# Plain products in the first quarter and a root on GpSimd, in a kernel of linear attention and two feed-forward layers

## The chip, the cores and the metric

The kernel runs on one core of a Trainium2 chip. The time is that of one execution on the device, in microseconds (us); of the kernel before three runs were made, and their median counts. The traces come from the hardware profiler: they record, for each engine, when every instruction began and how long it took.

## The reference

Four batches of eight heads, 576 tokens each and 64 wide, go through linear attention with a norm; the 2,304 rows of 512 numbers that come out go through two feed-forward layers, 512 to 2048 to 512 each.

```
kv  = einsum('bhsd,bhse->bhde', k, v)
out = einsum('bhsd,bhde->bhse', q, kv)
rms = sqrt(mean(out * out, axis=-1) + 1e-06)
x   = (out / rms * g_norm), rows of all heads side by side     # 2304 x 512
h   = x @ w_in;   g = max(h, 0) + log1p(exp(-|h|));  x = g @ w_out    # layer 1
h   = x @ w_in2;  g = h if h > 0 else exp(h) - 1;    y = g @ w_out2   # layer 2
```

The weights come as 64-bit floats. Attention is computed in fp32. In the layers every operand is split into a high and a low part of a shorter format, and a product is the sum of three: high by high, high by low, low by high.

## The kernel before

**Tiles.** The tokens form 18 tiles of 128 rows, three to a block of 384, six blocks, two blocks to a pair. d_ff is cut into four quarters. A slot is one step of a layer: one pair of blocks by half a quarter (256 columns for the first block and 256 for the second, in two halves each); 24 slots make a layer, numbered s, two to a pair and six to a quarter.

**Products of a slot.** A slot's first matrix product is done as two by two blocks by the scheme of Strassen and Winograd: seven products instead of eight (`OPS`, in the order 1, 6, 7, 5, 4, 2, 3), each of six matmuls of 384 columns (`product`, L650) into banks A, B and C. Their operands are blocks of x or sums of such blocks: op 1, 2, 4 are a11, a12, a22 of the pair as they are, 6, 7, 5, 3 are sums (`operands`: sums L588 and L596, high part L602 on ScalarE, low part L614 on VectorE, 768 elements wide). In the first quarter they are made in SBUF and spilled to memory (L620); later quarters read them back (L609). The banks are added on VectorE (L688) before the activation. The second matrix product follows in plain pieces (L840 to L842), three matmuls each, fitted between the first products of a later slot. `x`, `whi`, `wlo` and `wx` in the trace are these operands and the weights' high, low and summed parts; numbers at their names are layer, quarter, pair, op or layer's chunk and half.

**Attention.** Per batch and head pair c, `kv_strand` loads k and v and makes ten small matmuls (L388) and copies the result to `kvf` (L403). Tiles of the first block are done four times by head pairs (`('pair', c)`, 384 wide), all later ones tile by tile (512 wide). `attention` is a chain through all engines: product on TensorE (L422), squares on ScalarE (L429), their sum over each head on VectorE (L433, into `small`, 8 numbers a row), Ln and Exp on ScalarE for the reciprocal root (L437, L439), one Newton step to sharpen it in five GpSimd instructions (L442 to L446), scaling on VectorE (`y`, L450, reading the product from PSUM and the root from SBUF), transposes on TensorE (L459) and a copy on ScalarE (L464) into the block's x in `acc_sb`.

**Weights.** `conv` loads 64-bit words into one of three `raw` rooms (L257) and builds 32-bit floats: two passes on ScalarE, four on VectorE (L272, L276, L281, L285); `split` and its relatives make the parts (L303 on ScalarE, L307 on VectorE). Ln and Exp need one table of ScalarE and softplus another: the second is loaded when all 19 roots are through (in `softplus`).

**Order.** Every engine runs its own queue in order. The queues are written out by a planner, `Order`: each piece of work is a strand with a key; from the strands whose needs are met (marks, and rooms of rings that have come free) it takes the one that can start first on its engine, the lower key going ahead, by its own prices for matmuls, DMAs and the rest. TensorE is given small matmuls on the identity (`warm`, L898) where it would stand still; in the trace they are `warm<-kvf`, `warm<-ident` and `A<-ident`, two records each. All DMAs are issued by SyncE's queue.

Of the kernel before, what the change touches and what calls it, by code (L numbers as in the profile page):

```python
# [41 lines left out]
def dma(nbytes):  # L42
    return nbytes / 360


class Order:
# [9 lines left out]
    DMA_LATENCY = 1000  # L56
# [15 lines left out]
    def add(self, key, strand):  # L72

        s = [key, strand, None, self.end if self.strands else 0.0]
# [24 lines left out]
    def when(self, need):  # L99

        if callable(need):
            return 0.0 if need() else None
# [16 lines left out]
    def run(self):  # L119
        while self.strands:  # L120
            heads = {}
            for s in self.strands:
                at = s[3]
                for need in s[2][1]:
# [3 lines left out]
                    at = max(at, w)  # L128
# [3 lines left out]
            if not heads:  # L132
                stuck = [(s[0], s[1].gi_code.co_name, [n for n in s[2][1] if self.when(n) is None]) for s in self.strands]
                raise RuntimeError(f"no strand can go on: {stuck[:9]}")
# [12 lines left out]
            self.end = done + (self.DMA_LATENCY if e == DMA else self.LATENCY)  # L147
            s[3] = self.end if e != PE else done
            self.now, self.going = s[0], s
# [10 lines left out]
def linear_attention_then_two_ffns(  # L160
# [41 lines left out]
    OPS = (1, 6, 7, 5, 4, 2, 3)  # L202
    EPS = 1e-6
# [48 lines left out]
    def conv(i):  # L252
        layer, fc, half = chunks[i]
        n = f"{layer}_{fc}_{half}"
        yield ((DMA, dma(P * 4096)),), [ring("raw"), ("load", i - 1)]
        raw, raw_h = sbuf("raw", 3, f"raw{n}", dtype=I64, uses=2)
# [36 lines left out]
    def split(i, n):  # L293
# [5 lines left out]
        if half == 0 and fc % 2 == 0:  # L299
# [37 lines left out]
    def split_sums(layer, fc, wx, wx_h, ct, ct_h, rt, rt_h):  # L337
# [17 lines left out]
    roots = []  # L355
    TILES = NP + NTT - TT


    made_of = [
        [t for t in range(TT, NTT) if t * P < (b + 1) * S and (t + 1) * P > b * S] for b in range(B)  # L360
    ]
    made_of[0] += [("pair", c) for c in range(NP)]

    ROOM = {"sx": 7, "wx": 2, "gx": 3}

    def kv_room(b, c):


        if b < 2:
            return acc_sb[NB - NP + c], None  # L370
        return sbuf("gx", ROOM["gx"], f"kv_sb{b}_{c}", (P, T * KC))

    def kv_strand(b, c):
        n, r = 4 * 2 * D2, S - 4 * P
        yield ((DMA, dma(4 * n * P)),), ([], [("kvmm", 0, c)], [ring("gx")])[min(b, 2)]
        t, t_h = kv_room(b, c)
# [3 lines left out]
        old = [("po", t) for t in made_of[b - 2]] if b > 1 else []  # L380
        tag = "om"[c % 2]
        yield ((PE, 5 * 165),), [ring(tag), *old]
# [13 lines left out]
        if t_h:  # L396
            drop(t_h)
# [11 lines left out]
    def attention(nm, load, products, n, parts):  # L409

        h = n // D
        yield ((DMA, dma(P * n * 4)),), [ring("qt")]
        q, q_h = sbuf("qt", 3, f"q{nm}", (P, NP, P))
        load(q)

        yield ((PE, sum(pe(P, 4) for _ in products)),), [
            ring("acc"),
            *{("kv", b, c) for b, c, *_ in products},
        ]
        bank, po_h = psum("acc", f"po{nm}")  # L420
        for b, c, rows, cols, lhs in products:
            nc.tensor.matmul(bank[rows, cols], lhs(q), kvf[b % 2][:, c, :], start=True, stop=True)  # L422
        drop(q_h)
# [3 lines left out]
        sq, sq_h = sbuf("e", 2, f"sq{nm}")  # L427
        sq = sq[:, :n]
        nc.scalar.activation(sq, po, AF.Square)  # L429
# [3 lines left out]
        nc.vector.reduce_sum(ms, sq.rearrange("p (h e) -> p h e", h=h), axis=AX.X)  # L433
        drop(sq_h)

        yield ((ACT, 100),), []
        nc.scalar.activation(r, ms, AF.Ln, scale=1.0 / D, bias=EPS)  # L437
        yield ((ACT, 100),), []
        nc.scalar.activation(r, r, AF.Exp, scale=-0.5)  # L439
        roots.append(nm)  # L440
        yield ((POOL, 5 * 280),), []
        nc.gpsimd.tensor_scalar(m, ms, 1.0 / D, EPS, op0=ALU.mult, op1=ALU.add)  # L442
        nc.gpsimd.tensor_mul(u, r, r)
        nc.gpsimd.tensor_mul(u, u, m)
        nc.gpsimd.tensor_scalar(u, u, -0.5, 1.5, op0=ALU.mult, op1=ALU.add)
        nc.gpsimd.tensor_mul(r, r, u)  # L446
        yield ((DVE, dve(n)),), [ring("G")]
        y, y_h = sbuf("G", 4, f"y{nm}")
        y = y[:, :n]
# [11 lines left out]
        j, pt, x = parts(po)  # L461
        old = [("kvmm", 1, j - NB + NP)] if j >= NB - NP else []
        yield ((ACT, act(n, True) + 90),), [("gn",), *old]
        nc.scalar.activation(x, pt, AF.Copy, scale=gn)  # L464
        drop(po_h)
        mark("x", nm)

    def pair_strand(c):


        def load(q):
            nc.sync.dma_start(q[:, :TT, :], qt[:TT, :, c, :].rearrange("t p n -> p t n"))

        def parts(pt):
            return 0, pt, acc_sb[0][:, c * T : (c + 1) * T]

        products = [
            (0, c, slice(0, P), slice(t * D2, (t + 1) * D2), lambda q, t=t: q[:, t, :])
            for t in range(TT)
        ]  # L480
        return attention(("pair", c), load, products, T, parts)

    def tile_strand(t):


        def load(q):
            nc.sync.dma_start(q, qt[t])

        def parts(pt):
            j, o = divmod(t, TT)  # L490
            tok = slice(o * P, (o + 1) * P)
            x = acc_sb[j].rearrange("p (c t) -> p c t", c=KC)
            return j, pt.rearrange("p (c t) -> p c t", c=KC), x[:, :, tok]

        products = []
        s = 0
        while s < P:
            b = (t * P + s) // S
            e = min(P, (b + 1) * S - t * P)
            for c in range(NP):  # L500
                cols = slice(c * D2, (c + 1) * D2)
                products.append((b, c, slice(s, e), cols, lambda q, c=c, s=s, e=e: q[:, c, s:e]))
            s = e
        return attention(t, load, products, DM, parts)

    def block_sum(layer, q, j, i, w0, w1, p, p_h):
# [5 lines left out]
        if q == 0:  # L512

            old = [("xop", layer, 0, j // 2, o) for o in OPS]
# [12 lines left out]
        else:  # L527
            yield ((DVE, dve(w)),), [ring("qt")]
            o, o_h = sbuf("qt", 3, f"o{j}_{i}_{w0}", (P, NP, P))
            o = o.rearrange("p c t -> p (c t)")[:, :w]  # L530
# [25 lines left out]

    def operand(layer, q, p, o):
        t = sbuf("sx", ROOM["sx"], f"x{layer}_{q}_{p}_{o}", (P, 4, T), F32R, uses=2 - (q > 0))
        op_t[layer, q, p, o] = t
        return t[0]  # L560

    def operands(layer):
# [3 lines left out]
        W = 2 * T  # L566
        for p in range(NPAIR):
            order.rekey(base(SLOTS * layer + FP * p) - X_LEAD)
            if layer == 0 and p == 0:
                order.rekey(FIRST)  # L570
            top, low = acc_sb[2 * p], acc_sb[2 * p + 1]
            a11, a12, a21, a22 = top[:, :W], top[:, W:], low[:, :W], low[:, W:]

            def made(b):
                j = 2 * p + b
                if layer:
                    return [("y", layer - 1, j, i) for i in range(KC)]
                if j == 0:
                    return [("x", ("pair", c)) for c in range(NP)]
                return [("x", t) for t in range(j * TT, (j + 1) * TT)]  # L580

            need = made(0)
            s1 = None
            for o in OPS:
                if o == 6:
                    yield ((DVE, dve(W)),), [ring("s1"), *made(1)]
                    s1, s1_h = sbuf("s1", 1, f"s1_{layer}_{p}", (P, W))
                    nc.vector.tensor_add(s1, a21, a22)  # L588

                sums = {  # L590
                    6: [(a21, a11, a21, []), (a11, s1, a11, [("xop", layer, 0, p, 1)])],
                    3: [(a12, a12, a11, [("xop", layer, 0, p, 2)])],
                }
                for to, x, y, old in sums.get(o, []):
                    yield ((DVE, dve(W)),), old
                    nc.vector.tensor_sub(to, x, y)  # L596
                of = {1: a11, 6: a11, 7: a21, 5: s1, 4: a22, 2: a12, 3: a12}
                yield ((ACT, act(W)),), [ring("sx"), *need]
                need = []
                t = operand(layer, 0, p, o)  # L600
                x = of[o].rearrange("p (k t) -> p k t", k=2)
                nc.scalar.copy(t[:, :2, :], x)  # L602
                order.add(order.now, low_part(layer, p, o, t, x, s1_h if o == 5 else None))
        for q in range(1, NQ):
            for p in range(NPAIR):
                order.rekey(base(SLOTS * layer + FP * (NPAIR * q + p)) - X_LEAD)
                for o in OPS:
                    yield ((DMA, dma(P * 4 * T * 4)),), [ring("sx"), ("spilled", layer, p, o)]
# [3 lines left out]
    def low_part(layer, p, o, t, x, x_h):  # L612
# [3 lines left out]
        if x_h:  # L616
            drop(x_h)
        order.rekey(max(order.now, SPILL))
# [42 lines left out]

    def slot_h(s, pieces):
# [341 lines left out]
```

## Time and profile before

| | |
|---|---|
| median of three runs | 844.22 us (843.2 to 846.75) |
| the profiled execution | 843.19 us, of which its span is 841.1 |
| TensorE matmuls (PE) | busy 824.6 us, 98% of the span |
| weight loads of TensorE (PEld) | 778.9, 93% |
| VectorE (DVE) | 600.2, 71% |
| ScalarE (ACT) | 466.1, 55% |
| GpSimd (POOL) | 29.9, 4% |

Busy time of TensorE is modelled where matmuls are pipelined. The span runs from the first instruction to the last; what the execution takes beyond it can't be seen in the trace. GpSimd works in the first 85 us only, where attention is; the two layers' products fill the rest.

### The profile page before, as it was taken

What the parts mean: (1) busy time and instruction counts of PE and PEld (TensorE: products, weight loads), DVE (VectorE), ACT (ScalarE), POOL (GpSimd) and SP (SyncE); (2) the same over time, 40 slices, a digit from 0 to 9 for tenths busy, and PEclk for the clock granted to TensorE, in tenths of its full rate; (3) what the DMA queues carried; (4) which work ended last, traced back from release to release, by engine and by line L of the source; (5) the groups of instructions that cost most, each with busy time, mean ns of one, the idle gap of its engine ahead of it and who ended that gap; (6) DMA issues with size and microseconds to landing.
All of it is one profiled execution on the core that took longest, in us unless ns stands there. A gap on an engine that the chain in (4) does not pass through costs nothing.

```text
span 841.1 us, 12584 instructions
## 1 busy us (share of the span) xinstructions
PE 824.6 (98%) x4814; PEld 778.9 (93%) x4814; DVE 600.2 (71%) x986; ACT 466.1 (55%) x826; POOL 29.9 (4%) x101
## 2 busy tenths in 40 slices
PE   8889999999999999999999999999999999999998
PEld 7778999999999999999999988988988888898897
DVE  2778988866458855778379999888678875865444
ACT  4667767656234633455256767677455654654341
POOL 1425000000000000000000000000000000000000
PEclk9999999999999999999999999999999999999999
DMA  8877747855735853855716447845844954753713
GB/s 279 281 278 278 273 153 300 314 189 224 288 125 213 336 178 138 312 191 200 285 60 254 172 178 303 310 173 221 307 172 151 328 199 151 252 180 130 290 38 113
DMA packets 43707, 185.36 MB, mean 220 GB/s; under 512 B 4992, under 2 KB 7808, under 8 KB 43648
## 3 DMA queue, kind: packets, MB, share of 16 engines
q1 hardware_dynamic: 43648, 184.57, 60.5%
q8 instruction: 38, 0.62, 0.3%
q14 instruction: 21, 0.17, 0.1%
HBM read 146.80 MB, written 37.75 MB: 219 GB/s over the span
## 4 chain that ended last, share of the span: by engine, by line
PE 93%; DMA 4%; SPq 1%; ACT 1%; issue 0%; POOL 0%; DVE 0%; ACTq 0%; DVEq 0%
PE A L650 24%; PE acc L841 16%; PE acc L842 16%; PE acc L840 16%; PE B L650 12%; PE C L650 6%; PE A L898 2%; DMA acc_sb<-kv 1%; DMA kv_sb<-kv 1%; DMA raw<-w 1%; PE po L422 1%; DMA q<-qt 1%; PE kv L388 1%; PE po L459 0%; SPq L379 0%
## 5 line engine op out<-in xcount | busy, mean ns | idle before, releaser
L840 PE MATMUL acc<-G,whi 128*128 128x384 f32 x384 | 128.5, 335 | 0.0
L841 PE MATMUL acc<-G,wlo 128*128 128x384 f32 x384 | 128.3, 334 | 0.0
L842 PE MATMUL acc<-G,whi 128*128 128x384 f32 x384 | 128.3, 334 | 0.0
L650 PE MATMUL A<-x,wx 128*128 128x384 f32 x576 | 116.9, 337 | 0.1
L841 PE MATMUL acc<-whi,G 128*128 128x512 f32 (+1 forms) x292 | 114.5, 392 | 0.7 <-DVE G L802 0.7
L842 PE MATMUL acc<-wlo,G 128*128 128x512 f32 (+1 forms) x292 | 114.9, 393 | 0.0
L650 PE MATMUL A<-x,whi 128*128 128x384 f32 x384 | 113.1, 335 | 0.0
L840 PE MATMUL acc<-whi,G 128*128 128x512 f32 (+1 forms) x292 | 112.7, 386 | 0.0
L650 PEld LDWEIGHTS A<-x,wx 128*128 128x128 f32 x576 | 102.5, 189 | 4.7 <-ACT hj L678 0.8
L688 DVE TENSOR_TENSOR hk<-hk,B 128x384 f32<-128x384 f32 x48 | 26.5, 553 | 75.1 <-PE B L650 65.2
L688 DVE TENSOR_TENSOR hj<-hj,C 128x384 f32<-128x384 f32 x48 | 26.6, 554 | 69.6 <-PE C L650 69.4
L650 PEld LDWEIGHTS A<-x,whi 128*128 128x128 f32 x384 | 70.8, 188 | 1.8
L841 PEld LDWEIGHTS acc<-G,wlo 128*128 128x128 f32 x384 | 72.1, 188 | 0.1
L840 PEld LDWEIGHTS acc<-G,whi 128*128 128x128 f32 x384 | 72.1, 188 | 0.0
L842 PEld LDWEIGHTS acc<-G,whi 128*128 128x128 f32 x384 | 72.1, 188 | 0.0
L842 PEld LDWEIGHTS acc<-wlo,G 128*128 128x128 f32 x292 | 54.7, 187 | 11.3
L523 DVE TENSOR_TENSOR acc_sb<-acc_sb,acc 128x384 f32<-128x384 f32 (+1 forms) x108 | 62.3, 596 | 3.7 <-PE acc L842 2.0
L650 PE MATMUL A<-x,wlo 128*128 128x384 f32 x192 | 64.4, 335 | 0.0
L841 PEld LDWEIGHTS acc<-whi,G 128*128 128x128 f32 x292 | 54.8, 188 | 7.0 <-DVE G L802 1.1
L840 PEld LDWEIGHTS acc<-whi,G 128*128 128x128 f32 x292 | 54.9, 188 | 6.0
L650 PE MATMUL B<-x,wx 128*128 128x384 f32 x288 | 58.2, 336 | 0.0
L303 ACT CAST whi<-q 128x512 fp32r<-128x512 f32 x64 | 39.7, 620 | 32.4 <-DVE q L285 14.3
(149 smaller groups left out, 1545.0 us busy)
## 6 DMA issues: line engine op xcount, KB each, us to landing
x<-spill SPq DMA_DIRECT2D x126, 768.0 KB, 5.8
raw<-w SPq DMA_DIRECT2D x64, 512.0 KB, 5.6
spill<-x SPq DMA_DIRECT2D x42, 768.0 KB, 5.3
out<-o SPq DMA_DIRECT2D x17, 256.0 KB, 2.0
acc_sb<-kv SPq DMA_DIRECT2D x8, 512.0 KB, 5.2
kv_sb<-kv SPq DMA_DIRECT2D x8, 512.0 KB, 5.0
q<-qt SPq DMA_DIRECT2D x15, 256.0 KB, 5.0
acc_sb<-kv_rest SPq DMA_DIRECT2D x8, 64.0 KB, 4.5
```

The costliest lines, as they stand in the source:

```text
L303: nc.scalar.copy(hi, q)
L388: nc.tensor.matmul(p[i * D : (i + 1) * D, :D], t[:r, o + i * D : o + (i + 1) * D], t[:r, o + D2 + i * D : o + D2 + (i + 1) * D], start=(n ...
L422: nc.tensor.matmul(bank[rows, cols], lhs(q), kvf[b % 2][:, c, :], start=True, stop=True)
L523: nc.vector.tensor_add(a, a, p)
L650: nc.tensor.matmul(bank[:, :T], w, x, start=start and i == 0, stop=stop and i == len(seq) - 1, skip_group_check=True,)
L688: nc.vector.tensor_add(to, to, bank[:, :T])
L840: nc.tensor.matmul(a, l[0], r[0], start=(u == 0), stop=False)
L841: nc.tensor.matmul(a, l[1], r[0], start=False, stop=False)
L842: nc.tensor.matmul(a, l[0], r[1], start=False, stop=(u == QF - 1))
L898: nc.tensor.matmul((chain[0] if chain else p)[:, -P:], a, a, start=not chain, stop=not chain, skip_group_check=True)
```

## The change

**Plain products in the first quarter.** The six slots of layer 1's first quarter do eight plain products (`slot_plain`, `plain_product`, `plain_act`), with operands a11, a12, a21 (a new op 8) and a22. The four sums are made later by a second strand (`make` with ops 6, 7, 5, 3) and only spilled. Activations read the two halves' banks directly; the bank additions on VectorE fall away in these slots. Sums of weights (`wx`) aren't made for this quarter.

```
+    PLAIN_OPS = (1, 2, 8, 4)
...
+    def plain_product(s, b, c, half):
...
+        o = ((1, 2), (8, 4))[b][half]
+        need = [("xop", layer, q, p, o), ("w", layer, 2 * f + c, 0)]
...
+    def slot_plain(s, pieces):
...
+        for b in range(2):
+            for c in range(2):
+                for half in range(2):
+                    yield from plain_product(s, b, c, half)
+                if b or c:
+                    yield from some_of(pieces, 4)
+            order.add(base(s) + H_KEY + b, plain_act(s, b))
...
+            if layer == 0:
+                order.rekey(X_KEY[p])
+                order.add(X_SUMS[p], make(layer, p, (6, 7, 5, 3)))
+            else:
+                order.rekey(base(SLOTS * layer + FP * p) - X_LEAD)
+            yield from make(layer, p, OPS if layer else PLAIN_OPS)
```

**Attention.** The first two blocks are now done by head pairs, eight units (j, c) with Ln, Exp and five GpSimd instructions as before. The twelve tiles of blocks 2 to 5 get their first guess of the root from the number's bits, by two VectorE instructions of 8 elements, and three Newton steps of four GpSimd instructions. So the softplus table waits for eight roots instead of 19. The squares are written where y will stand, in the ring e, which has three rooms instead of two.

```
+        if first:
...
+            nc.gpsimd.tensor_scalar(m, ms, -0.5 / D, -0.5 * EPS, op0=ALU.mult, op1=ALU.add)
+            steps = 1
+        else:
+
+            yield ((DVE, 100),), []
+            nc.vector.tensor_scalar(m, ms, -0.5 / D, -0.5 * EPS, op0=ALU.mult, op1=ALU.add)
+            yield ((DVE, 100),), []
+            nc.vector.tensor_scalar(
+                r.bitcast(U32), m.bitcast(U32), -0.5, float(0x9EF759DF), op0=ALU.mult, op1=ALU.add
+            )
+            yield ((POOL, 12 * 280),), []
+            steps = 3
+        for _ in range(steps):
+            nc.gpsimd.tensor_mul(u, r, r)
+            nc.gpsimd.tensor_mul(u, u, m)
+            nc.gpsimd.tensor_scalar(u, u, 1.5, None, op0=ALU.add)
+            nc.gpsimd.tensor_mul(r, r, u)
```

**Rooms and order.** The q tiles of the first three blocks are loaded early into rooms that x operands use later, the first two raw weights into the rooms of wx and the next three into those of the ring gx, the kv loads into `acc_sb` of blocks 2 to 5; the raw ring has two rooms instead of three. The planner's prices and keys change, and output pieces of slots 2 to 7 may be taken wherever TensorE would stand still (`Pieces`, `filler`).

```
-    return nbytes / 360
+    return nbytes / 320
...
-    DMA_LATENCY = 1000
+    DMA_LATENCY = 2000
+    PE_LATENCY = 250
...
+        tag = "wx" if i < 2 else "gx" if i < 5 else "raw"
...
+    KV_AT = [[2, 3, 4, 5]] * 2 + [[4, 5, 4, 5]] * 2
...
+    KV_KEY = (-20, -18, -5, 2)
+    UNIT_KEY = (-19.9, -17.9, -9, -4, 4, 5)
...
+    X_KEY = (-19, 2, 8)
+    X_SUMS = (1.5, 9, 17)
```

What this does to the queues is seen at three places. First TensorE around its first wide product. The rows give the line, the operation, output and inputs, the size and, behind an x, how many such matmuls follow each other. In the program before, kv and po rows belong to the second batch and the tiles that need it:

```order
L422 MATMUL po_456<-kvf_69,q_425 128x128 x4
L388 MATMUL kv_0_473<-kv_sb_0_410 64x64 x10
L388 MATMUL kv_1_491<-kv_sb_1_438 64x64 x10
L459 MATMUL po_401<-ident,y_502 128x128 x4
L388 MATMUL kv_2_522<-kv_sb_2_453 64x64 x10
L422 MATMUL po_537<-kvf_69,q_489 128x128 x4
L459 MATMUL po_433<-ident,y_545 128x128 x4
L388 MATMUL kv_3_559<-kv_sb_3_511 64x64 x10
L898 MATMUL warm<-ident 128x128
L650 MATMUL A_591<-x_0_0_1_462,whi_0_0_520 128x384
```

In the changed program the names in brackets are block and head pair:

```order
L417 MATMUL kv_0_298<-acc_sb_72 64x64 x10
L529 MATMUL po(0, 2)_231<-ident,y(0, 2)_237 128x128 x3
L1059 MATMUL warm<-ident 128x128 x10
L529 MATMUL po(0, 3)_263<-ident,y(0, 3)_281 128x128 x3
L1059 MATMUL warm<-ident 128x128
L480 MATMUL po(1, 0)_350<-kvf_68,q_269 128x128
L480 MATMUL po(1, 0)_350<-kvf_68,q_269 64x128
L480 MATMUL po(1, 0)_350<-kvf_69,q_269 64x128
L480 MATMUL po(1, 0)_350<-kvf_69,q_269 128x128
L1059 MATMUL warm<-ident 128x128 x3
L734 MATMUL A_0_0_369<-x_0_0_1_311,whi_0_0_355 128x384
```

The first wide product moved ahead of most of the second batch's kv matrices and of all tiles behind block 1.

Second TensorE at the longest row of fillers before, in slot 2, between the first product of pair 1 and the first output piece (acc):

```order
L650 MATMUL A_1168<-x_0_1_1_1071,wlo_0_0_572 128x384
L650 MATMUL A_1168<-x_0_1_1_1071,whi_0_0_520 128x384 x2
L898 MATMUL A_1168<-ident 128x128 x27
L840 MATMUL acc_0_0_1_0_1239<-G_1_0_1143,whi_0_1_1224 128x384
L841 MATMUL acc_0_0_1_0_1239<-G_1_0_1143,wlo_0_1_1232 128x384
```

At the same product in the changed program:

```order
L952 MATMUL acc_0_0_0_3_1032<-G_0_0_679,whi_1_1_916 128x384
L953 MATMUL acc_0_0_0_3_1032<-G_0_0_679,wlo_1_1_929 128x384
L954 MATMUL acc_0_0_0_3_1032<-G_0_1_680,whi_1_1_916 128x384
L1059 MATMUL A_1_1_998<-ident 128x128 x5
L734 MATMUL A_0_0_1092<-x_0_1_1_859,whi_0_0_355 128x384
```

Output pieces of the first block now stand ahead of pair 1's first product, and five fillers where 27 were.

Third VectorE where tiles meet the weights. In the program before, y (L450) comes between the passes of the weights (L272 to L285):

```order
L272 TENSOR_SCALAR c_2_0_792<-raw_2_0_688 128x512
L433 TENSOR_REDUCE small_801<-sq_785 128x8
L276 SCALAR_TENSOR_TENSOR c_2_0_792<-raw_2_0_688,c_2_0_792 128x512
L450 TENSOR_TENSOR y_820<-po_537,small_757 128x512
L433 TENSOR_REDUCE small_831<-sq_803 128x8
L450 TENSOR_TENSOR y_838<-po_604,small_769 128x512
L281 ISA c_2_0_792<-c_2_0_792,r_2_0_715 128x1024
L450 TENSOR_TENSOR y_859<-po_697,small_801 128x512
```

In the changed program small_577 and small_597 are the first two tiles of block 2, L509 is the last instruction ahead of their GpSimd chains and L520 their y:

```order
L509 TENSOR_SCALAR small_577<-small_577 128x8
L509 TENSOR_SCALAR small_597<-small_597 128x8
L493 TENSOR_REDUCE small_629<-y_620 128x8
L282 TENSOR_SCALAR c_3_0_647<-raw_3_0_474 128x512
L507 TENSOR_SCALAR small_629<-small_629 128x8
L286 SCALAR_TENSOR_TENSOR c_3_0_647<-raw_3_0_474,c_3_0_647 128x512
L509 TENSOR_SCALAR small_629<-small_629 128x8
L291 ISA c_3_0_647<-c_3_0_647,r_3_0_614 128x1024
L295 SCALAR_TENSOR_TENSOR q_3_0_615<-q_3_0_615,c_3_0_647 128x512
L520 TENSOR_TENSOR y_530<-po_491,small_577 128x512
L622 TENSOR_TENSOR s_0_0_708<-acc_sb_71 128x768
L317 TENSOR_TENSOR wlo_3_0_719<-q_3_0_615,whi_3_0_706 128x512
```

Two tiny instructions precede each chain, and behind each y stand sums of operands (L622, L634), their low parts (L668) and the weights' parts (L317).

## Rows read from the trace of the kernel before

**Rows 1.** The core: span and mean granted clock of TensorE.

```profile
core 0: 841.1 us, clock 0.998
```

**Rows 2.** Windows: length; busy us (instructions) of PE, PEld, DVE, ACT, POOL; clock; DMA.

```profile
0.00:60.00 60.00, 50.37 (x565) 44.66 (x566) 33.30 (x53) 34.30 (x97) 16.76 (x59) 0.97 0.85 281
118.00:194.40 76.40, 76.40 (x443) 76.40 (x442) 57.42 (x93) 53.08 (x97) 0.00 (x0) 1.00 0.70 259
194.40:841.10 646.70, 642.97 (x3421) 604.82 (x3419) 457.69 (x760) 335.36 (x550) 0.00 (x0) 1.00 0.57 208
60.00:110.00 50.00, 46.89 (x339) 45.08 (x338) 44.21 (x71) 36.82 (x74) 13.09 (x43) 1.00 0.74 274
```

**Rows 3.** Timeline of TensorE: start, length, engine, line, form [idle before]; fillers, cut.

```profile
90.95 5.85 PE L898 MATMUL A<-ident 128*128 128x128 f32 x50 [0.57 <-ACT hj L678]
96.56 0.42 PE L840 MATMUL acc<-G,whi 128*128 128x384 f32 x1
...
193.34 0.33 PE L840 MATMUL acc<-G,whi 128*128 128x384 f32 x1
...
194.38 0.33 PE L650 MATMUL A<-x,whi 128*128 128x384 f32 x1
```

**Rows 4.** The same, first 40 us.

```profile
10.21 0.95 PE L388 MATMUL kv<-acc_sb 128*64 128x64 f32 x20 [1.48 <-DMA acc_sb<-kv]
...
18.54 0.95 PE L388 MATMUL kv<-acc_sb 128*64 128x64 f32 x20 [0.20 <-DMA acc_sb<-kv]
...
19.96 1.06 PE L422 MATMUL po<-kvf,q 128*128 128x128 f32 x8
...
28.96 0.66 PE L459 MATMUL po<-ident,y 128*128 128x128 f32 x4
...
39.47 0.42 PE L650 MATMUL A<-x,whi 128*128 128x384 f32 x1
```

**Rows 5.** Timeline of VectorE at two places.

```profile
39.17 0.96 DVE L588 TENSOR_TENSOR s<-acc_sb 128x768 f32<-128x768 f32 x1 [0.50 <-ACT acc_sb L464]
40.05 0.42 DVE L326 TENSOR_TENSOR t<-q,q 128x256 f32<-128x256 f32 x1
...
62.35 0.69 DVE L450 TENSOR_TENSOR y<-po,small 128x512 f32<-128x512 f32 x1
62.96 0.68 DVE L285 SCALAR_TENSOR_TENSOR q<-q,c 128x512 f32<-128x512 f32 x1
```

**Rows 6.** Groups of VectorE: busy us, mean ns of one | idle before them.

```profile
L272 DVE TENSOR_SCALAR c<-raw 128x512 uint32<-128x512 uint32 x64 | 26.9, 421 | 0.0
L450 DVE TENSOR_TENSOR y<-po,small 128x512 f32<-128x512 f32 x15 | 10.3, 689 | 3.5 <-POOL small L446 3.1
L332 DVE TENSOR_TENSOR q<-q,t 128x256 f32<-128x256 f32 x16 | 6.8, 425 | 0.5
```

**Rows 7.** Timeline of GpSimd at the same two places.

```profile
39.56 0.63 POOL L443 TENSOR_TENSOR small<-small 128x8 f32<-128x8 f32 x1 [1.79 <-ACT small L439]
...
43.78 0.20 POOL L446 TENSOR_TENSOR small<-small 128x8 f32<-128x8 f32 x1
...
62.68 0.20 POOL L443 TENSOR_TENSOR small<-small 128x8 f32<-128x8 f32 x1
62.95 0.74 POOL L444 TENSOR_TENSOR small<-small 128x8 f32<-128x8 f32 x1
```

**Rows 8.** Windows of two us, columns as in the second group: two gaps of TensorE.

```profile
26.00:28.00 2.00, 0.53 (x6) 0.56 (x8) 1.21 (x3) 0.66 (x1) 1.11 (x3) 1.00 1.06 418
...
54.00:56.00 2.00, 2.00 (x23) 1.76 (x19) 0.39 (x1) 1.93 (x7) 0.07 (x1) 0.50 1.02 402
56.00:58.00 2.00, 2.00 (x10) 2.00 (x9) 1.29 (x2) 1.97 (x8) 0.34 (x2) 0.66 0.56 230
```

More of the change, by code (lines that the diff above doesn't have):

```diff
@@ L101, in when @@
         if callable(need):
[L102 removed]
+            return need()
         if need[0] != "ring":
@@ L127, in run @@
                         break
-                    at = max(at, w)
+                    late = slack and w > 0 and need[0] not in ("load", "spilled")
+                    at = max(at, w + (slack if late else 0.0))
                 else:
@@ L298, in split @@
         q, q_h = q_t.pop(i)
-        if half == 0 and fc % 2 == 0:
+        if half == 0 and fc % 2 == 0 and (layer or fc >= QF):
             q_h[0] += 1
@@ L407, in kv_strand, with q_strand @@
         mark("kv", b, c)
-    def attention(nm, load, products, n, parts):
-        h = n // D
[L412 to L423, printed above, removed]
+    def q_strand(t):
+        j, i = divmod(t, TT)
+        early = j < 3
+        yield ((DMA, dma(P * DM * 4)),), [ring("sx") if early else ring("qt")] if not early or i == 0 else []
+        if not early:
+            tile_q[t] = sbuf("qt", QT, f"q{t}", (P, NP, P))
+        elif i == 0:
+            q, q_h = sbuf("sx", ROOM["sx"], f"q{j}", (P, TT, NP, P), uses=len(units(j)))
+            for i in range(TT):
+                tile_q[t + i] = q[:, i], q_h
+        nc.sync.dma_start(tile_q[t][0], qt[t])
+        mark("tile", t)
@@ new lines, in attention @@
+    def attention(nm):
+        first = isinstance(nm, tuple)
+        if first:
+            j, c = nm
+            products = [
+                (b, c, slice(s, e), slice(i * D2, (i + 1) * D2), j * TT + i)
+                for i in range(TT)
+                for b, s, e in batches(j * TT + i)
+            ]
+            n = T
+            x = acc_sb[j][:, c * T : (c + 1) * T]
+            tag = "acc"
+        else:
+            j, o = divmod(nm, TT)
+            products = [
+                (b, c, slice(s, e), slice(c * D2, (c + 1) * D2), nm)
+                for b, s, e in batches(nm)
+                for c in range(NP)
+            ]
+            n = DM
+            x = acc_sb[j].rearrange("p (c t) -> p c t", c=KC)[:, :, o * P : (o + 1) * P]
+            tag = "acc" if j < 3 else "om"[nm % 2]
+        h = n // D
+        need = dict.fromkeys([("kv", p[0], p[1]) for p in products] + [("tile", p[4]) for p in products])
+        yield ((PE, sum(pe(P, 4) for _ in products)),), [ring(tag), *need, *room_free(j, B, 0)]
+        bank, po_h = psum(tag, f"po{nm}")
+        for b, c, rows, cols, t in products:
+            nc.tensor.matmul(
+                bank[rows, cols], tile_q[t][0][:, c, rows], kvf[b % 2][:, c, :], start=True, stop=True
+            )
+        drop(tile_q[products[0][4]][1])
@@ L460, in attention @@
         drop(y_h)
[L461 to L464, printed above, removed]
+        yield ((ACT, act(n, True) + 90),), [("gn",)]
+        nc.scalar.activation(x, po if first else po.rearrange("p (c t) -> p c t", c=KC), AF.Copy, scale=gn)
         drop(po_h)
         mark("x", nm)
[L468 to L504, printed above, removed]
     def block_sum(layer, q, j, i, w0, w1, p, p_h):
@@ L562, in operands @@
     def operands(layer):
-        W = 2 * T
         for p in range(NPAIR):
[L568 to L603, printed above, removed]
@@ L860, in linear_attention_then_two_ffns, with __init__, __bool__, ready @@
     W_LEAD2 = 8
-    KV_LEAD = 2
-    FIRST = -14.5
-    SECOND = -7.5
+    KV_KEY = (-20, -18, -5, 2)
+    UNIT_KEY = (-19.9, -17.9, -9, -4, 4, 5)
+    W_IN_FIRST = (-18.5, -11)
+    W_OUT_FIRST = (-3, -1)
+    X_KEY = (-19, 2, 8)
+    X_SUMS = (1.5, 9, 17)
     SPILL = 1
     WARM_SLOTS = 7
+    FILLED = 8
+    QT = 3
     chain = []
+    class Pieces:
+        def __init__(self, pieces):
+            self.pieces = pieces
+            self.head = None
+        def __bool__(self):
+            if not self.head:
+                piece = next(self.pieces, None)
+                self.head = piece and (piece, *next(piece))
+            return bool(self.head)
+        def ready(self):
+            if not self:
+                return 0.0
+            at = [order.when(n) for n in self.head[2]]
+            return None if None in at else max(at)
+        def take(self):
+            if self:
+                piece, self.head = self.head[0], None
+                next(piece, None)
+    def one(pieces):
+        if pieces:
+            yield pieces.head[1], [pieces.ready]
+            pieces.take()
+    def some_of(pieces, n):
+        for _ in range(n):
+            yield from one(pieces)
+    def filler():
+        for s in range(FP, FILLED):
+            while pieces_of[s]:
+                yield from one(pieces_of[s])
+    pieces_of = {}
     def main():
-        pieces = {}
         groups = LAYERS * SLOTS // FP
@@ L880, in main @@
                 entry[0] = base(s)
-            left = pieces.get(s, iter(()))
-            if s < LAYERS * SLOTS:
+            left = pieces_of.get(s, Pieces(iter(())))
+            if s < FP * NPAIR:
+                yield from slot_plain(s, left)
+            elif s < LAYERS * SLOTS:
                 yield from slot_h(s, left)
-            for piece in left:
-                yield from piece
+            while left:
+                yield from one(left)
     def warm():
         p, p_h = psum("h", "warm")
-        while entry[0] < base(WARM_SLOTS):
+        for _ in range(2000):
+            if entry[0] >= base(WARM_SLOTS):
+                break
             yield ((PE, pe(P, 4)),), []
-            a = ident if ("x", ("pair", 0)) in order.marks else kvf[1][:, 0, :]
+            a = ident if ("x", (0, 0)) in order.marks else kvf[1][:, 0, :]
             if chain and p_h:
```

237 lines of the change are left out of this document (168 added, 69 removed).

## The prediction, made before the changed kernel was run

> **What bounds the kernel now.** I read the span and clock first: 841.1 us at 0.998 [rows 1]. The profiled execution took 843.19, so 2.1 lie outside the span; the median of the runs shown, 844.22, is 1.0 above the profiled one. Then the windows by stage [rows 2]. From 118 us on TensorE is busy for 76.40 of 76.40 us, and behind 194.40 for 642.97 of 646.70: nothing but matmuls counts there. Of the first 60 us it is busy for 50.37 only, part of that with fillers. So I cut the program at one instruction that both kernels have, the first product of quarter 2, pair 1 (operand x_1_1_1). Before reaches it at 194.38 [rows 3]. Behind it the two programs' TensorE queues are the same, instruction for instruction; I leave the rest at 841.1 − 194.4 = 646.7 us. The question is when the changed kernel gets there.
>
> **Prices.** On a saturated TensorE six matmuls of 384 columns start in 194.38 − 193.34 = 1.04 us, 0.1735 each; the 25 fillers of the long pause (two records each) take 96.56 − 90.95 = 5.61, 0.224 each [rows 3]. A set of attention products takes 1.0, four transposes 0.6, the ten products of a kv matrix 0.88 (starts and lengths in [rows 4]). A VectorE instruction over 512 elements starts 0.61 behind the one before (62.35 to 62.96), one over 768 0.88 (39.17 to 40.05) [rows 5]; a 512-element scalar form takes 0.42 [rows 6]. GpSimd's small instructions start 0.28 apart undisturbed (62.68 to 62.95) [rows 7].
>
> **Plain products and fillers.** Six slots of eight products instead of seven: 36 matmuls more, 6.2 us. Fillers fall from 109 to 73, 8.1 less. TensorE's work alone comes out near even, so what counts is what it waits for.
>
> **The start.** The first product stands at 39.47 [rows 4]. In the new order it follows the first product set of block 1, whose last input is the third q tile, behind 5 kv loads of 0.590 MB, 6 q tiles of 0.262 and 2 raw weights of 0.524: 5.57 MB. The trace's kv matrices that waited for their DMA started at 10.21 behind 2.16 MB and at 18.54 behind 4.72 [rows 4], 0.307 MB per us from 3.2 us on; so 21.3. The set (1.0), three fillers (0.7) and two VectorE instructions (1.4, the weight's and the operand's low parts, whose cover I can't show) give 24.4. Ends: 23.0 without the two, 30 if all eight early kv loads (7.34 MB, 27.1) must land first.
>
> **The root on GpSimd.** This decides. Twelve tiles now run 2 tiny VectorE instructions and a chain of 12 GpSimd ones each, where 5 were, and y waits for the chain in VectorE's in-order queue, ahead of the operands' low parts and the weights. The tiny ones (8 elements) are not in the trace; the smallest there, 256 elements, takes 0.425 [rows 6]; on the line from 0.69 at 512 over 0.425 at 256 I take 0.15, with 0 and 0.42 as ends (21 of them: −3 to +6 us).
>
> What a chain costs the trace shows well. A GpSimd instruction that meets a VectorE one with two operands in SBUF ends with it: L444 takes 0.74 from 62.95, while L285 runs from 62.96 for 0.68; beside L450, which reads one of its operands from PSUM, L443 takes its 0.20 [rows 5, 7]. In the densest stretch nine of them take 43.78 + 0.28 − 39.56 = 4.5 us, 0.50 each [rows 7].
>
> The first tile's chain can start when VectorE has done 26 instructions behind the first product. At the pace of 60 to 110 us (71 in 50.00, 0.704 each [rows 2]) that is 24.4 + 18.3 = 42.7. (Ends: 37.5 at the bare spacings, 13.1 us, and 48 with the late start.) From there to the twelfth tile's y VectorE has 113 instructions in its queue: 29 over 768 elements (25.5 us), 54 over 512 (32.9), 8 scalar forms (3.5), 21 tiny (3.2), one of 0.5, in all 65.6. Walking both queues row by row with the hold above, 44 of the twelve chains' 144 GpSimd instructions are held, 19 at 0.88 and 25 at 0.61; the other 100 take 0.28. A chain comes to 5.1 us, and when VectorE arrives at y some six instructions are still to come: a wait of 1.76 on average, 21.1 for twelve (in the trace of before 15 such products wait 3.1 in all [rows 6]). So the last y ends at 42.7 + 65.6 + 21.1 = 129.4.
>
> Is TensorE there by then? From 46 us (the first activation, 3 us behind the first chain's start, when the eighth root is through and the softplus table in, frees its banks) it has 282 wide matmuls (186 plain, 96 output; 48.9 us), ten sets (10.0), eleven of transposes (6.6), six kv matrices (5.3) and 14 fillers (3.1) up to that transpose, 73.9 us: by its own list it is there at 120. It waits for y. Behind the twelfth transpose (0.6) come 354 matmuls, 61.4. The cut is reached at 129.5 + 62.0 = 191.5, 2.9 before today's 194.4. The operands of pair 2 are there (133.9) just as TensorE wants them (134.3).
>
> A rule bears on the hold: the Trainium skill, SBUF — State Buffer, section "Who interferes with whom", says that a VectorE instruction with two SBUF inputs and a GpSimd one that reads SBUF exclude each other, and that whoever issues first holds the pair for the whole instruction. The first half is what the rows show. By the second L285, issued 0.01 behind L444, would have waited for it; it started 0.61 behind its forerunner as always [rows 5], so GpSimd yields here. By the rule some 24 runs of two-input instructions, meeting a chain in flight 0.7 of the time with 0.1 us left, would add 1.7; I add nothing.
>
> **Early rooms, smaller rings, planner's prices.** Raw weights have two rooms instead of three, the e ring three instead of two; the planner's new DMA prices only order the queues. From 194.4 on the DMA share is 0.57 [rows 2], so I cost them nothing; if a weight is late there, a stall of 1 to 3 us.
>
> **Clock.** Fewer fillers leave short gaps. One gap of before was followed by clocks of 0.50 and 0.66 (1.7 us lost in 54 to 58), in the other, at 26 to 28 with 0.53 busy, the clock stayed 1.00 [rows 8]. I take half of one loss, 0.8; ends 0 and 5 (three losses). [...]
>
> **Sum.** 191.5 + 646.7 + 0.8 = 839.0 span, + 2.1 = 841.1 as a profiled execution (before 843.2), + 1.0 = **842.1** median. In general 821.0 + 12w, with w the mean wait of y for GpSimd.
>
> **The rivals.**
> (A) The chain stays hidden and TensorE's own list is the bound. For it: before's products wait for GpSimd 3.1 us in all [rows 6], and the order gives each y three to eight instructions of cover; against it: its chains were 5 long, and the holds above. From 46 us: 29.6 us of work to pair 1 (72 plain matmuls 12.5, 24 output 4.2, 3 sets 3.0, 6 transposes 3.3, 4 kv 3.5, 14 fillers 3.1), then 106 to the cut (540 matmuls 93.7, 7 sets 7.0, 6 transposes 3.5, 2 kv 1.8): cut at 181.6, 832.2 us.
> (B) The start comes forward by less: the first product at 30, everything 5.6 later, 847.7, about the same. For it: DMA already runs at a share of 0.85 in the first 60 us [rows 2]; against it: the order asks for q and weights before the second batch's kv.
> (C) Slower: GpSimd beside a full VectorE at the densest stretch's 0.50 each [rows 7]: 6.0 us a chain, w 2.6, 10.3 us more, 852.4. It decides from w = 2.28 (848.4). For it: VectorE's queue has a two-input instruction in 61 of 113 places; against it: while VectorE stands waiting for y, nothing holds GpSimd.
> That the change doesn't do what it says gets no chance: its instructions have the 12 GpSimd rows of every later tile, and no Ln or Exp for one.
>
> **Chances.** The forecast 0.46 (its own range 837 to 847), A 0.25, B 0.12, C 0.17. A change under 0.5% (4.2 us) is about what a measurement of this kernel can't tell from none: 840.0 to 848.4 is the same. Of the forecast 0.13 lie under 840.0 (w under 1.58, or an earlier chain) and 0.33 in the band; A is all faster; of B 0.10 are in the band and 0.02 above; C is slower. So faster 0.38, same 0.43, slower 0.19. The range of 8 in 10 reaches from A's lower part to half of C: 831 to 851.
>
> **What would show it.** First product near 24 (over 28: B). GpSimd's twelve instructions of a tile in about 5.1 us, with those beside two-input VectorE instructions 0.5 to 0.9 long; VectorE idle before L520 about 1.8 us a tile, put down to GpSimd (under 0.5: A; over 2.3: C). The twelfth tile's y near 129, TensorE idle before its transposes, the cut at 191.5, and 646.7 behind it; were that stretch different by over 3 us, the cut was no fair one.

## The result and the profile after

The changed kernel takes 851.78 us (four runs, 851.2 to 852.54) against 843.95 for the kernel before beside it (four runs, 843.2 to 846.75): a ratio of 1.0087, with a 95% interval from 1.0063 to 1.0112. It is slower by about 8 us; forecast were 842.1 and no clear change, and the range ended at 851.0. Each of the later ratios is to the kernel before as measured beside that run (843.6 to 845.2 us).

Core, first wide product, the twelfth later tile's transposes and the cut, in the changed kernel (the timeline's columns are start, length, engine, line, form, idle before; they answer to [rows 1, 3, 4]):

```profile
core 0: 850.0 us, clock 0.998
```

```profile
25.30 0.42 PE L734 MATMUL A<-x,whi 128*128 128x384 f32 x1
...
139.12 0.66 PE L529 MATMUL po<-ident,y 128*128 128x128 f32 x4 [0.78 <-DVE y L520]
...
203.25 0.33 PE L706 MATMUL A<-x,whi 128*128 128x384 f32 x1
```

The reader is to see three distances. The first product moved from 39.47 to 25.30. The cut moved the other way, from 194.38 to 203.25, 8.9 later. Behind it 850.0 − 203.25 = 646.75 us are left, as before (646.7). So all of the loss lies between 25 and 203 us, and 14 us of head start are given back there and 9 more.

The window of the stretch from the first later chain to the last y, columns as in [rows 2]:

```profile
43.66:139.06 95.40, 79.78 (x581) 72.77 (x580) 66.59 (x113) 57.23 (x105) 52.41 (x144) 0.98 0.61 222
```

TensorE stands for 15.6 of 95.4 us, and every other engine is idle for longer: they wait for each other. 14.1 of TensorE's 15.6 us lie ahead of the transposes (L529) and are put down to y. VectorE's groups in the same stretch say what VectorE itself waits for (busy, mean ns | idle before them and its releaser):

```profile
L668 DVE TENSOR_TENSOR x<-acc_sb,x 128x768 fp32r<-128x768 f32 x12 | 11.4, 955 | 2.1 <-ACT x L640 2.1
L520 DVE TENSOR_TENSOR y<-po,small 128x512 f32<-128x512 f32 x12 | 8.3, 692 | 20.0 <-POOL small L518 20.0
L493 DVE TENSOR_REDUCE small<-y 128x8 f32<-128x512 f32 x10 | 6.8, 680 | 3.0 <-ACT y L489 3.0
L317 DVE TENSOR_TENSOR wlo<-q,whi 128x512 fp32r<-128x512 f32 x8 | 5.5, 693 | 1.9 <-ACT whi L313 1.9
```

y waits 20.0 us for GpSimd where it waited 3.1 [rows 6]. The rest of the idle, 95.4 − 66.6 − 20.0 = 8.8 us, is mostly put down to ScalarE (7.0).

One chain of GpSimd, and VectorE beside it:

```profile
91.67 0.84 POOL L515 TENSOR_TENSOR small<-small 128x8 f32<-128x8 f32 x1 [13.40 <-DVE small L509]
92.59 0.80 POOL L516 TENSOR_TENSOR small<-small 128x8 f32<-128x8 f32 x1
93.47 0.94 POOL L517 TENSOR_SCALAR small<-small 128x8 f32<-128x8 f32 x1
94.49 0.88 POOL L518 TENSOR_TENSOR small<-small 128x8 f32<-128x8 f32 x1
95.45 0.20 POOL L515 TENSOR_TENSOR small<-small 128x8 f32<-128x8 f32 x1
...
96.02 0.23 POOL L517 TENSOR_SCALAR small<-small 128x8 f32<-128x8 f32 x1
...
97.50 0.20 POOL L518 TENSOR_TENSOR small<-small 128x8 f32<-128x8 f32 x1
```

```profile
91.50 0.95 DVE L914 TENSOR_TENSOR G<-hk,G 128x768 fp32r<-128x768 f32 x1
92.37 0.95 DVE L622 TENSOR_TENSOR s<-acc_sb 128x768 f32<-128x768 f32 x1
93.36 0.96 DVE L634 TENSOR_TENSOR acc_sb<-acc_sb,acc_sb 128x768 f32<-128x768 f32 x1
94.35 0.96 DVE L634 TENSOR_TENSOR acc_sb<-s,acc_sb 128x768 f32<-128x768 f32 x1
97.74 0.69 DVE L520 TENSOR_TENSOR y<-po,small 128x512 f32<-128x512 f32 x1 [2.43 <-POOL small L518]
```

Four of twelve instructions end with one of VectorE's two-input instructions, and the eight left over make y wait 2.43 us. Undisturbed, the scalar form L517 takes 0.23 us and the others 0.20. Of the 144 in the twelve chains 50 took clearly longer than that (over 0.255).

### The profile page after: what moved, and what is told of

Its sections match the earlier page's. It is cut to its first block, busy times and chain, and to the rows that moved or that the text cites. A ratio compares the mean times of both kernels' runs of the same rounds, so it can differ in the third digit from the quotient of the medians.

```text
span 850.0 us, 12537 instructions
## 1 busy us (share of the span) xinstructions
PE 825.4 (97%) x4778; PEld 774.5 (91%) x4778; DVE 594.6 (70%) x988; ACT 457.0 (54%) x790; POOL 65.5 (8%) x190
## 4 chain that ended last, share of the span: by engine, by line
PE 80%; ACT 0%; issue 0%; DVE 0%; DVEq 0%
PE A L706 21%; PE acc L953 15%; PE acc L954 15%; PE acc L952 14%; PE B L706 10%; PE C L706 5%; PE A L734 1%; DVE G L914 0%; ACT x L640 0%; ACT G L912 0%; ACT r L276 0%; ACT whi L313 0%; ACT acc_sb L547 0%; DVE o L561 0%; ACT hk L775 0%
## 5 line engine op out<-in xcount | busy, mean ns | idle before, releaser
L706 PE MATMUL A<-x,wx 128*128 128x384 f32 x504 | 101.2, 335 | 0.0
L706 PE MATMUL A<-x,whi 128*128 128x384 f32 x336 | 98.8, 334 | 0.4 <-ACT hk L775 0.4
L706 PEld LDWEIGHTS A<-x,wx 128*128 128x128 f32 x504 | 89.3, 188 | 4.3 <-ACT hj L795 0.5
L805 DVE TENSOR_TENSOR hk<-hk,B 128x384 f32<-128x384 f32 x42 | 23.3, 554 | 76.0 <-PE B L706 56.3
L954 PEld LDWEIGHTS acc<-wlo,G 128*128 128x128 f32 x292 | 54.7, 187 | 11.3
L805 DVE TENSOR_TENSOR hj<-hj,C 128x384 f32<-128x384 f32 x42 | 23.3, 554 | 58.9 <-PE C L706 58.8
L706 PEld LDWEIGHTS A<-x,whi 128*128 128x128 f32 x336 | 61.9, 188 | 2.6 <-ACT hk L775 0.8
L313 ACT CAST whi<-q 128x512 fp32r<-128x512 f32 x64 | 39.7, 620 | 34.0 <-DVE q L342 11.3
L734 PE MATMUL A<-x,whi 128*128 128x384 f32 x192 | 56.3, 350 | 1.5 <-ACT hj L775 1.3
L706 PE MATMUL A<-x,wlo 128*128 128x384 f32 x168 | 56.4, 336 | 0.0
```

Of the source, the lines that this page charges most:

```text
L313: nc.scalar.copy(hi, q)
L706: nc.tensor.matmul(bank[:, :T], w, x, start=start and i == 0, stop=stop and i == len(seq) - 1, skip_group_check=True,)
L734: nc.tensor.matmul(a[:, :T], w, x, start=half == 0 and i == 0, stop=half == 1 and i == len(seq) - 1, skip_group_check=True,)
L805: nc.vector.tensor_add(to, to, bank[:, :T])
L954: nc.tensor.matmul(a, l[0], r[1], start=False, stop=(u == QF - 1))
```

## The experiments

Theory 1: y waits in VectorE's queue for the chain, and all other engines wait for y. Theory 2: the plain products and the new start cost the time, and the chain is only what is named. In the first three runs the order of the queues is the changed kernel's and only the chain's length differs.

**Two Newton steps.** `-            steps = 3` / `+            steps = 2`

> Left out: the third Newton step of the twelve later tiles (8 GpSimd instructions a tile instead of 12, the order of all queues unchanged), so the root is less exact. Theory 1 (y waits in VectorE's queue for the GpSimd chain, and TensorE waits for y): the four unheld instructions at a chain's end go, 4 x 0.28 = 1.1 us a tile, 13.4 us of the 20.0 that y waits; the cut comes at 190 to 193 instead of 203.25, 839 to 842 us, unless TensorE's own list (cut near 182 to 185) comes first. Theory 2 (the loss is in the plain products and in waits on ScalarE and TensorE; the chain is only what ends last): 850 to 853.

Measured: 837.53 us, ratio to before 0.9915 (0.9900 to 0.9930), 14.3 less than with three steps and somewhat under the 839 to 842 that I had expected.

**One step.** `+            steps = 1`

> Left out: the second and third Newton step of the twelve later tiles (4 GpSimd instructions a tile), queues in the same order. Theory 1: y no longer waits, 20 us of VectorE's idle time go, and TensorE's own list is what is left: cut at 182 to 187, 831 to 836 us. Theory 2: 850 to 853. If the loop over ScalarE and TensorE (7.7 us of VectorE's waits) stays by itself, it ends no earlier than with two steps.

Measured: 833.7 us, 0.9870 (0.9855 to 0.9885); the cut stands at 184.82.

**Four steps.** `+            steps = 4`

> Added: a fourth Newton step in the twelve later tiles (16 GpSimd instructions a tile), queues in the same order. Theory 1: each tile's y comes 4 x 0.28 = 1.1 us later, 13.4 us in all: 865 us. Theory 2: 852 to 855.

Measured: 867.85 us, 1.0278 (1.0261 to 1.0296), 16.1 more than with three (expected: 865). The wait of y with one, two and four steps:

```profile
L520 DVE TENSOR_TENSOR y<-po,small 128x512 f32<-128x512 f32 x12 | 8.2, 682 | 0.1
```

```profile
L520 DVE TENSOR_TENSOR y<-po,small 128x512 f32<-128x512 f32 x12 | 8.3, 691 | 5.9 <-POOL small L518 5.6
```

```profile
L520 DVE TENSOR_TENSOR y<-po,small 128x512 f32<-128x512 f32 x12 | 8.3, 691 | 33.3 <-POOL small L518 33.3
```

From 5.9 us over 20.0 to 33.3 the time goes from 837.5 over 851.8 to 867.9: 1.0 and 1.2 us for each us of waiting; with four steps the granted clock was lower, too, 0.92 from the first later chain to the last y against 0.98 with three. From 0.1 to 5.9 it is 0.7. TensorE's waits for y ahead of its transposes are 14.9 us in the changed kernel as a whole and none, 3.2 and 25.8 with one, two and four steps. Theory 2 is out: with the plain products and the new start left as they are, the kernel is 1.3% faster than before once y does not wait. With one step TensorE is busy for 94.6 of the 95.4 us in which it was for 79.8, so its own list is what is left:

```profile
43.66:139.06 95.40, 94.59 (x685) 89.45 (x684) 82.83 (x137) 69.55 (x128) 24.76 (x47) 1.00 0.73 265
```

The same run shows that slow GpSimd instructions by themselves cost nothing: 32 of its 48 are held (the four lines' means are 0.38 to 0.63 us, two of them below), and y still doesn't wait, as the order gives it other work for that long.

```profile
L517 POOL TENSOR_SCALAR small<-small 128x8 f32<-128x8 f32 x12 | 7.5, 626 | 1.0
...
L515 POOL TENSOR_TENSOR small<-small 128x8 f32<-128x8 f32 x12 | 4.5, 377 | 50.9 <-DVE small L509 50.9
```

**The planner's price.** The planner sets y where it believes the chain to end, at 280 ns an instruction; the trace has 52.41 us / 144 = 364 ns, with the 0.08 us between two of them some 445. Only the price is changed, and so the order:

```
-            yield ((POOL, 12 * 280),), []
+            yield ((POOL, 12 * 430),), []     # and 350, and 520
```

> Only the planner's price of the chain is changed, from 280 to 430 ns an instruction (what they took in the trace, with their gaps), so the queues are put in another order. Theory 1: y is put further back, other work of VectorE covers the chain, y's waits fall from 20 us to under 8 and the time to 842 to 848. Theory 2: no gain, 850 to 855.

Measured: 837.38 us, 0.9915 (0.9898 to 0.9931), better than the 842 to 848 that I had expected.

> The planner's price of the chain alone, 350 ns an instruction instead of 280 (430 gave 837.4 us, y waiting 6.6; the trace has 445 with gaps). Theory 1: y's waits between those of 280 and 430, near 12 us, and the time in step: 841 to 846. If what counts is another accident of the order and not the price's fit, the time falls outside 836 to 852.

Measured: 844.6 us, 1.0008 (0.9994 to 1.0021): as fast as before.

> The same at 520 ns, above what the chain takes: 86 fillers instead of 72. Theory 1: y waits under 4 us, but the order now holds TensorE's pieces back behind a y that has long been there; no faster than 430: 836 to 841.

Measured: 837.54 us, 0.9920 (0.9891 to 0.9950). The wait of y at 350, 430 and 520:

```profile
L520 DVE TENSOR_TENSOR y<-po,small 128x512 f32<-128x512 f32 x12 | 8.3, 692 | 16.0 <-POOL small L518 16.0
```

```profile
L520 DVE TENSOR_TENSOR y<-po,small 128x512 f32<-128x512 f32 x12 | 8.3, 691 | 6.6 <-POOL small L518 6.5
```

```profile
L520 DVE TENSOR_TENSOR y<-po,small 128x512 f32<-128x512 f32 x12 | 8.2, 687 | 2.1 <-POOL small L518 1.7
```

With the same instructions, all twelve of each chain, the order alone is worth 14.4 us. At 350 I had expected a wait of 12 us; it was 16.0, and the time fell by 7.2 us although VectorE's wait fell by 4.0 only. A new order moves other work, too: VectorE's other waits from the first later chain to the last y come to 4.2 us there instead of 8.8. TensorE's waits for y ahead of its transposes fit better: 7.2, 2.2 and 0.2 us at 350, 430 and 520, after 14.9. So from 430 to 520 VectorE's wait falls by another 4.5 us and the time stays, since TensorE hardly waits for y any more.

**The old root in the changed kernel, the new root in the kernel before.** The two halves of the exchange alone. In the first all 20 units take Ln and Exp, and the softplus table waits for 20 roots; in the second the 15 later tiles of before take the new root, in before's order.

```
-        if first:
+        if True:
...
-            yield ((ACT, 1300),), [lambda: 0.0 if len(roots) == FIRST_BLOCKS * NP else None]
+            yield ((ACT, 1300),), [lambda: 0.0 if len(roots) == FIRST_BLOCKS * NP + NTT - FIRST_BLOCKS * TT else None]
```

> The changed kernel with the old root for all 20 units (Ln and Exp on ScalarE, five GpSimd instructions), so that the softplus table waits for 20 roots; the order follows from that, with 215 fillers instead of 73. Theory 1: y hardly waits for GpSimd (under 3 us), but no plain product's bank is freed before the last root, near 75 us: 860 to 875. Theory 2: 850 to 855, as the plain products are there as before.

Measured: 871.48 us, 1.0314 (1.0262 to 1.0366). y waits 7.3 us in all, not under 3, and the last root comes later than the 75 us I had expected: ScalarE loads the softplus table at 107.25, in the changed kernel at 44.45, and only then comes the first activation that frees a plain product's bank. ScalarE in the changed kernel, then in this run:

```profile
44.45 1.28 ACT L234 ACT_TABLE_LOAD   x1
```

```profile
107.25 1.28 ACT L234 ACT_TABLE_LOAD   x1
108.55 0.87 ACT L775 ACTIVATE hj<-A 128x384 f32<-128x384 f32 x2
```

```
+        else:
+            yield ((ACT, 100),), []
+            nc.vector.tensor_scalar(m, ms, -0.5 / D, -0.5 * EPS, op0=ALU.mult, op1=ALU.add)
...
+            yield ((POOL, 5 * 280),), []
+            steps = 3
```

> The kernel before with the new root alone: its 15 later tiles get the two small VectorE instructions and 12 GpSimd ones in place of Ln, Exp and five; all else, the order of the queues included, as before. Theory 1 (the chain holds up y and so VectorE and TensorE): a chain is 7 instructions longer, 2.0 to 3.1 us, less the two ScalarE instructions and their waits (1 to 2): y's waits rise from 3.1 us to 15 or more and the time to 850 to 860. Theory 2 (the plain products and the new start cost the time): 843 to 846.

Measured: 869.92 us, 1.0289 (1.0244 to 1.0333), more than the 850 to 860 I had expected.

```profile
L463 DVE TENSOR_TENSOR y<-po,small 128x512 f32<-128x512 f32 x15 | 10.4, 692 | 31.2 <-POOL small L459 31.2
```

y waits 31.2 us instead of 3.1, and the softplus table, at its old place in ScalarE's queue, is loaded at 104.15 instead of 80.78. A lower clock lies on top: 0.87 from 0 to 120 us,

```profile
0.00:40.00 40.00, 32.88 (x342) 28.71 (x342) 13.00 (x28) 17.53 (x48) 12.29 (x50) 0.87 0.77 249
40.00:80.00 40.00, 31.09 (x270) 27.27 (x270) 24.97 (x51) 20.65 (x43) 25.43 (x84) 0.87 0.69 238
80.00:120.00 40.00, 27.41 (x169) 25.48 (x170) 26.03 (x54) 19.57 (x33) 18.20 (x72) 0.87 0.34 120
```

that is 0.13 of 120 us, 15.6. How much of this lies in stretches in which TensorE had work I didn't separate. So each half by itself costs some 25 us (26.3 and 24.7): the plain products need the early table and so the new root, and the new root, in an order that wasn't made for it, is held up by its chains.

**The chain on VectorE.** The Trainium skill, GPSIMD Engine Reference, section "4.1 Engine selection", names VectorE for elementwise work and GpSimd as about half as fast for two inputs. Nine instructions instead of twelve (add and multiply in one):

```
+        for _ in range(0 if first else steps):
+            nc.vector.tensor_mul(u, r, r)
+            nc.vector.tensor_mul(u, u, m)
+            nc.vector.scalar_tensor_tensor(r, u, 1.5, r, op0=ALU.add, op1=ALU.mult)
+        for _ in range(steps if first else 0):
...
```

> The twelve tiles' three Newton steps run as nine VectorE instructions right behind the two small ones, none on GpSimd; queues otherwise in the same order. At 0.20 us each (as one L507 and L509 follow each other) 1.8 us a tile, 21.7 in all, in place of 20.0 us of waits and without holds. Theory 1, by VectorE's own work: 65.6 + 21.7 = 87 us to the last y against 95.4, 842 to 852 us according to how much of its waits on other engines stays. If the hold itself were no part of it and only work counted: 853.

Measured: 850.22 us, 1.0063 (1.0042 to 1.0085). No wait for GpSimd is left, and the time stays almost what it was:

```profile
L524 DVE TENSOR_TENSOR y<-po,small 128x512 f32<-128x512 f32 x12 | 8.2, 683 | 0.0
```

```profile
44.07 0.15 DVE L515 TENSOR_TENSOR small<-small 128x8 f32<-128x8 f32 x1
44.26 0.17 DVE L516 TENSOR_TENSOR small<-small 128x8 f32<-128x8 f32 x1
44.46 0.17 DVE L517 SCALAR_TENSOR_TENSOR small<-small 128x8 f32<-128x8 f32 x1
```

They start 0.20 us apart against 0.28 undisturbed on GpSimd [rows 7], so VectorE is the faster here too, though not twice as fast. But nine of them are 1.8 us a tile of VectorE's own queue, as much as y waited. GpSimd's own pace was not what bound the kernel; VectorE's queue was, and a late y is as late whether VectorE works ahead of it or waits. TensorE still waits 11.3 us for y ahead of its transposes, and between 40 and 120 us it is busy for 70.6 of 80 at a clock of 0.91.

**Two steps at the new price.** `yield ((POOL, 8 * 430),)`, `steps = 2`:

> Two Newton steps instead of three in the twelve later tiles (the third left out) and the planner's price of the chain at 8 x 430 ns, so that the order fits what a chain takes. Theory 1: y's waits under 3 us, TensorE's own list is the bound: 831 to 835. Theory 2: 845 or more.

Measured: 835.57 us, 0.9890 (0.9857 to 0.9922); y waits 3.5 us, a little more on both counts than the 835 and 3 that I had expected at most. The kernel before and the changed one are both beaten by this one and by one step in the unchanged order (833.7), which leave Newton steps out, and by the price of 430 alone (837.4), which leaves nothing out.

## Why the prediction was wrong

Right in size were these steps. The first product: 24.4 forecast, 25.30 measured, with some luck: its set of attention products began at 23.70 and not at 21.3, behind transposes that waited for the y of an earlier unit until 23.12, and the product stood 1.6 behind the set and not 3.1. The tiny instructions: 0.15, measured 0.168. The first later chain: 42.7, measured 43.66. A chain: 5.1 us (the prediction's own terms give 32.0 + 28.0 = 60.0 for twelve, 5.0 each), measured 5.3 on average, with 50 instructions held for 44 forecast. VectorE's work to the last y: 113 instructions, 65.6 us, measured 66.59. TensorE's own list to the twelfth transposes: 120, and 121.00 with one step, where it hardly waits. The waits of y: 21.1, measured 20.0. The rest behind the cut: 646.7, measured 646.75. That VectorE isn't held by GpSimd, against the second half of the rule that the Trainium skill, SBUF — State Buffer, section "Who interferes with whom", has on the shared pair: L286 and L291 take 688 and 687 ns on average in the stretch, against 690 and 689 for the same two in before (L276, L281). The clock: 0.8 us taken; this gap cost 1.7,

```profile
72.00:74.00 2.00, 1.75 (x23) 1.25 (x22) 1.93 (x5) 1.79 (x3) 0.97 (x2) 0.75 0.75 263
74.00:76.00 2.00, 2.00 (x10) 1.94 (x7) 2.00 (x4) 1.77 (x5) 1.75 (x4) 0.50 0.56 188
76.00:78.00 2.00, 2.00 (x12) 2.00 (x11) 0.16 (x1) 0.70 (x1) 1.50 (x7) 0.90 0.95 372
```

(0.25 + 0.50 + 0.10) x 2, and how much of it TensorE's next wait for y, 2.33 us before 98.48, made up isn't shown. After other waits it did not fall: from 96 to 100 us, with TensorE busy for 1.68 of 4.00, it stayed 1.00.

Wrong was the step "So the last y ends at 42.7 + 65.6 + 21.1 = 129.4". It ended at 139.06. The sum let VectorE wait for nothing but GpSimd: VectorE's waits for what ScalarE and TensorE hand it stood at nothing, without a reason, and they are the 8.8 us above. TensorE's list was walked by itself, and the later of two lists taken. But each of the two stops at places for the other, so waits on both sides count. The seventh tile shows it, ScalarE first, then TensorE and VectorE:

```profile
99.18 0.69 ACT L532 ACTIVATE acc_sb<-po,gn 128x512 f32<-128x512 f32 x1 [2.59 <-PE po L529]
99.77 1.46 ACT L547 COPY acc_sb<-acc 128x384 f32<-128x384 f32 x3
101.11 0.84 ACT L640 CAST x<-acc_sb 128x768 fp32r<-128x768 f32 x1
...
105.42 0.60 ACT L489 ACTIVATE y<-po 128x512 f32<-128x512 f32 x1 [0.55 <-PE po L480]
```

```profile
98.48 0.66 PE L529 MATMUL po<-ident,y 128*128 128x128 f32 x4 [2.33 <-DVE y L520]
...
103.80 2.67 PE L480 MATMUL po<-kvf,q 128*64 128x128 f32 x24
```

```profile
101.98 0.96 DVE L668 TENSOR_TENSOR x<-acc_sb,x 128x768 fp32r<-128x768 f32 x1 [1.82 <-ACT x L640]
102.86 0.42 DVE L282 TENSOR_SCALAR c<-raw 128x512 uint32<-128x512 uint32 x1
106.04 0.69 DVE L493 TENSOR_REDUCE small<-y 128x8 f32<-128x512 f32 x1 [2.76 <-ACT y L489]
```

The late y (97.74) holds TensorE's transposes for 2.33 us. ScalarE's copy waits 2.59 for them, the cast of an operand that had nothing to do with this tile stands behind the copy, and VectorE waits 1.82 for the cast. The products of the next tiles stand behind the transposes and other matmuls in TensorE's queue, so VectorE's sum over their squares waits 2.76.

It isn't y's lateness that makes these two waits. With one step, where y doesn't wait for its chain and ScalarE waits 0.26 instead of 2.59 for the transposes, both are the same to the hundredth:

```profile
86.99 0.69 DVE L520 TENSOR_TENSOR y<-po,small 128x512 f32<-128x512 f32 x1
...
91.24 0.96 DVE L668 TENSOR_TENSOR x<-acc_sb,x 128x768 fp32r<-128x768 f32 x1 [1.82 <-ACT x L640]
...
95.30 0.69 DVE L493 TENSOR_REDUCE small<-y 128x8 f32<-128x512 f32 x1 [2.76 <-ACT y L489]
```

```profile
88.43 0.69 ACT L532 ACTIVATE acc_sb<-po,gn 128x512 f32<-128x512 f32 x1 [0.26 <-PE po L529]
```

From y to this sum over squares it is 8.30 us with three steps and 8.31 with one: it hangs on what stands behind y in the queues of TensorE and ScalarE. From the first later chain to the last y VectorE's waits other than y's come to 11.1, 8.5, 8.8 and 11.7 us with one, two, three and four steps, while y waits 0.1, 5.9, 20.0 and 33.3. (With one step TensorE is busy for 76.3 of the stretch's 77.2 us, so VectorE's waits cost nothing there.) So the term left out is one that the order of the queues brings along, nearly the same whether y waits or not, and y's waits come on top of it. The trace of before had such waits as well: its low parts (L614) waited 3.9 us, nearly all of it for ScalarE. And for the way to the first chain the prediction had counted them: 0.704 us an instruction gave 18.3 us, measured 18.36. For the 113 it took bare spacings, 65.6 us, where they took 95.4 − 20.0 = 75.4 beside y's waits.

With 1.0 from the start and 2.1 behind the last y (203.25 − 139.12 = 64.1 instead of 62.0; the largest of TensorE's gaps there is 1.28 us before its product at 161.34, put down to ScalarE) the cut is missed by 11.8. Less the 0.8 that I had set apart for the clock that is 11.0 us of span (850.0 for 839.0); the median is off by 9.7, as the profiled execution was itself the median this time, not 1.0 below it, and had 1.8 outside the span.

The series of steps says the same: near the changed kernel a us of y's waiting costs 1.0 to 1.2, and the formula 821.0 + 12w is too low by 10.6, 10.8 and 13.6 us with two, three and four steps: it missed a nearly constant term and not a price on every wait. The 2.8 us more with four steps match VectorE's longer other waits there (11.7 for 8.8). The rivals: A's sum for TensorE's own list, 832.2, is close to what one step gave (833.7, cut at 184.82 for 181.6). C, slower by GpSimd, has the right sign and place, but not its price: a chain took some 0.445 an instruction and not 0.50, and w stayed at 1.67, under the 2.28 at which it was to decide.

What isn't settled: how the 10 to 11 us that the rest of the change gains (one step against before) divide between the earlier first product and the plain products; no run had one without the other. Nor was the hold taken away by itself: that VectorE's two-input instructions cause it rests on the rows. And no run took away VectorE's other waits alone; that the order sets them rests on the two rows of the seventh tile and on the price of 350.

## What to carry to other kernels

When a step goes from one in-order queue to a slower helper, walk the queues of all engines in the loop together: two lists that hand work to each other take longer than the longer of the two, as each stops for the other. A wait in a queue isn't mended by an engine with time to spare, but by what stands ahead of it: put the waiting instruction where the chain is done by measured durations, contention included. Here a planner's price, 280 to 430 ns, was worth 14.4 us with not one instruction less.

## What the runs showed of the hardware

Beside a full VectorE GpSimd's small instructions took 0.36 us on average and up to 0.94, against 0.20 (0.23 for the scalar form) alone, while VectorE's own kept their length (955 ns for the low parts in the stretch, 953 in the kernel before). The 8-element instructions on VectorE took 0.15 to 0.17 us and started 0.20 apart where each needed the one before.
